# Attention, routing and two feed-forward stages on one core: all queues of the attention loop in source order, not TensorE's alone

## The chip, the core and the metric

One core of a Trainium2 chip runs the whole program. Its engines have an instruction queue each: TensorE (matrix products and transposes, PE in the profile), VectorE (DVE), ScalarE (ACT), GpSimd (POOL) and SyncE (SP), which here only issues DMA and is the load queue. The metric is the time of one execution on the device in microseconds; lower is better.

## What is computed

The reference, cut to what matters (inputs in float32; 4 batches, 8 heads, 576 positions, head size 64):

```python
scores = scale * np.matmul(q, k.transpose(0, 1, 3, 2))
mask = (rel >= 0) & (rel < 64)              # rel = query position - key position
scores = np.where(mask, scores, -1000000000.0)
attn = np.exp(scores - np.max(scores, axis=-1, keepdims=True))
attn = attn / (np.sum(attn, axis=-1, keepdims=True) + 1e-09)
out = np.matmul(attn, v)                    # to rows: 2304 tokens x 512
...
noisy = x @ w_gate + np.log1p(np.exp(x @ w_noise)) * noise
# two best of 8 experts for each token, softmax over the two
out[mask] += top2_w[mask, k, None] * (np.maximum(x[mask] @ w1[e], 0.0) @ w2[e])
...
h = x @ w_in
out = (h * np.clip(h + 3.0, 0.0, 6.0) / 6.0) @ w_out
```

## The kernel before

The program has three parts: an attention loop with the routing of the first tokens woven in (about the first 135 us), the expert stage, and the feed-forward stage.

**The attention loop.** Two heads form a pair; there are 16 pairs of (batch, two heads). Each pair's 576 queries are cut into 9 chunks of 64, and three chunks make a group: 48 groups, numbered g, with n = g // 3 the pair and j = g % 3. A query sees at most its own chunk of keys and the one before. Around a group the loop body calls, in this order:

- `normalise` (odd g): VectorE takes the sums out of `pv`, inverts them (`rs`, L299, L300) and writes the scaled rows into `xbuf` (L304).
- `bg`: one step from a list `fill` of work for routing (below).
- `transposes(g)`: TensorE turns the exponentials `pb` of group g into `pt` (L255, three of them; one buffer).
- `exps(g + 1)`: ScalarE, three exponentials of the scores `s` with the negated maximum `mx` as bias (L247).
- `pt_copy(g)`: ScalarE copies `pt` to `ptb` (L260).
- `tr_half`: when j > 0, TensorE turns q or k of pair n + 2 (L212; two `tr` buffers), and ScalarE and VectorE copy them out (`qbd`, L220 and L222; `kt`, L226).
- `scores(g + 2)`: TensorE adds the mask and the products of q and k into `s` (L235, L239; two buffers), VectorE reduces the maximum `mx` (L241).
- `values(g - 2, g - 1)` (even g): TensorE, `ptb` times v into `pv` (L285).
- `bg` again, then `load_pair(n + 3)` on SyncE (q, k, v: L169, L172, L174; three buffers for q and k, four for v), `odd_slots(n + 2)` on GpSimd (the shifted copy of v, L156), and, for pairs 8 to 15 when j is 2, `w0q.step()`.

**Routing in the loop.** When a batch's heads are done, `gate_batch` adds a chain of steps to `fill`: each token tile is stored to `x_rows` (SyncE, L313), turned on TensorE (L316) and copied by ScalarE (`xT`, L318); then the products with the gate weights (L338), a copy `lt` on VectorE (L344), a turn back (L347), Exp and Ln on ScalarE (L355, L360) between small steps on VectorE (L354 to L370), the search for the two best (L375, L377), the place of each token (TensorE, L390 to L393, and a third Exp, L400), and pairs of one-hot tiles on VectorE (`pa`, L421; `pbt`, L422) whose products TensorE sums (L430). Two batches (token tiles 0 to 3 and 4 to 8) run whole within the loop, in the source at groups 13 to 26 and 27 to 41; then GpSimd gathers the first rows of expert 0 (L506) and TensorE turns them (L532, `build`) in group 45; the third batch begins in group 46 and ends in the expert stage.

**Weights of expert 0.** `w0q` holds eight weights, 512 KB each. A step settles the weight before (VectorE, low half = raw minus high half, L585), loads up to two ahead into two buffers `wraw` (SyncE, L567 or L571), and makes the next high half (GpSimd, L581). The eight steps stand at groups 26, 29, ... 47; the last low half (`lza`) is settled behind the loop. The expert stage begins with eight sums of twelve products each (L891 to L893) over the four weights `hwa`, `hxa`, `hya`, `hza`, then `hh` (ScalarE, L898) and `hl` (VectorE, L899).

**What sets the order.** The program is scheduled by a list scheduler: outside of a manual section it issues on each engine whichever instruction is ready first by its own estimates, source order deciding between ready ones. Inside `tc.manual_schedule(engines=...)` the engines named issue in the order of the source. The attention loop stands in such a section for TensorE alone; the set-up ahead of it stands in none; from the end of the loop on, a second section covers all engines:

```python
        w0q.step()
    order = ctx.enter_context(ExitStack())
    order.enter_context(tc.manual_schedule())
```

The two sections are separate: in the profile, products of the expert stage stand ahead of the last step of the loop's section on TensorE.

Of the kernel before, what the change touches and what calls it, by code (L numbers as in the profile page):

```python
# [40 lines left out]
def ap_of(t, offset, dims):  # L41
    return bass.AP(tensor=t.tensor, offset=t.offset + offset, ap=dims)
# [3 lines left out]
def attention_moe_kernel(ctx, tc, q, k, v, w_gate, w_noise, noise, w1, w2, w_in, w_out, out):  # L46
# [130 lines left out]
    def odd_slots(n):  # L177

        if n < NP:
            t = VT[n]  # L180
            pcopy(t[0:64, 1:8:2], t[64:128, 0:8:2])
            pcopy(t[64:128, 1:7:2], t[0:64, 2:8:2])
# [18 lines left out]
    def tr_half(n, which, a):  # L201
        if n >= NP:
            return
        raw = RAW[n, which]
        if n == 0 and which == "rk":
            tr = aps.tile([128, 3, 2, D + 1], F32, name="pv", bufs=2).rearrange("p c h n -> p (c h n)")
        else:
            tr = ps.tile([128, 512], F32, name="tr", bufs=2)
        r0, r1 = ((0, 4), (4, 6))[a]
        m, t0 = 96 * (r1 - r0), 96 * r0  # L210
        for r in range(r0, r1):
            pe.transpose(tr[:, 96 * (r - r0):96 * (r - r0) + 96], raw[:, r].rearrange("p h d -> p (h d)"), ident[0:96, 0:96])  # L212
        if which == "rq":

            t = QBD[n] = qbds[n % 2]
            for h in range(2):
                o = t[64 * h:64 * h + 64, t0 // 64:(t0 + m) // 64, h]
                i = tr[64 * h:64 * h + 64, 0:m].rearrange("p (c i) -> p c i", i=64)
                if a == 0:
                    act.activation(o, i, AF.Copy, scale=0.125)  # L220
                else:
                    dve.tensor_scalar(o, i, 0.125, None, op0=OP.mult)  # L222
        else:
            if a == 0:
                KT[n] = apool.tile([128, S], F32, name="kt", bufs=2)
            act.copy(KT[n][:, t0:t0 + m], tr[:, 0:m])  # L226
# [5 lines left out]
    def scores(g):  # L232
        n, cs = GROUPS[g]
        s = SC[g] = aps.tile([128, 3, 128], F32, name="s", bufs=2)
        pe.matmul(s, ident16, masks[:, 0:3] if cs[0] == 0 else masks[:, 1:4], start=True, stop=False)  # L235
        for i, c in enumerate(cs):
            l = QBD[n][:, c].rearrange("p h i -> p (h i)")
            k0 = 64 * max(c - 1, 0)
            pe.matmul(s[:, i, :], l, KT[n][:, k0:k0 + 128], start=False, stop=(i == 2))  # L239
        MX[g] = apool.tile([128, 3], F32, name="mx", bufs=3)  # L240
        dve.tensor_reduce(MX[g], s, axis=AX.X, op=OP.max, negate=True)  # L241

    def exps(g):
        n, cs = GROUPS[g]
        PB[g] = apool.tile([128, 3, 128], F32, name="pb", bufs=2)
        for i, c in enumerate(cs):
            act.activation(PB[g][:, i, :], SC[g][:, i, :], AF.Exp, bias=MX[g][:, i:i + 1])  # L247
# [40 lines left out]
    def normalise(g):  # L288
        n, cs = GROUPS[g]
        j = g % 3  # L290
        if j == 0:
            return
        b, p = divmod(n, HP)
        t0, odd = place_of(n, 0)
        pv = PV.pop((n, j - 1))
        m = 3 if j == 1 else 2
        spans = [(0, 1, 64, 128), (1, 3, 0, 128)] if odd and j == 1 else [(0, m, 0, 128)]
        rs = apool.tile([128, 3, 2], F32, name="rs", bufs=2)
        dve.tensor_scalar(rs[:, 0:m], pv[:, 0:m, :, D], 1e-9, None, op0=OP.add)  # L299
        dve.reciprocal(rs[:, 0:m], rs[:, 0:m])  # L300
        for u, w, lo, hi in spans:
            x0 = (t0 + 3 * (j - 1) + u) % (NT // 2)
            assert all(t < NT // 2 or t - NT // 2 in XT for t in range(t0 + 3 * (j - 1) + u, t0 + 3 * (j - 1) + w))
            dve.tensor_tensor(xbuf[lo:hi, x0:x0 + w - u, :, p].rearrange("q t (h a) y -> q t h a y", h=2),  # L304
                              pv[lo:hi, u:w, :, 0:D].rearrange("q t h (a y) -> q t h a y", a=2),
                              rs[lo:hi, u:w, :, None, None].to_broadcast([hi - lo, w - u, 2, 2, 32]), op=OP.mult)
# [194 lines left out]
    def gather(e, m):  # L501
        if e == 0:
            t = XG[e, m] = mp.tile([128, DM], F32, name="xg", bufs=4)
            early = m < SUBS[0][1]
            ix = idx0[:, m:m + 1] if early else idx[:, e, m:m + 1]
            pool.indirect_dma_start(out=t, out_offset=None,  # L506
                                    in_=xrows[0:128 * DONE[KNOWN][0]] if early else xrows,
                                    in_offset=bass.IndirectOffsetOnAxis(ap=ix, axis=0))
            return
        t = XG[e, m] = mp.tile([128, 4, 128], F32, name="xg", bufs=4)  # L510
        for i in range(4):
            pool.indirect_dma_start(out=t[:, i], out_offset=None, in_=pieces(xrows),  # L512
                                    in_offset=bass.IndirectOffsetOnAxis(ap=idx4[:, i, e, m:m + 1], axis=0))
# [26 lines left out]
    def build(e, m):  # L540
        if e == 0:
            s = int(m >= SUBS[0][1])
            turn_rows(XG[e, m], *columns(e, s), 128 * (m - SUBS[s][0]))
        elif m == 2:

            turn(XG[e, m], (*columns(e, 0), 0), (*columns(e, 1), 0))
        else:
            s = int(m > 2)
            turn(XG[e, m], (*columns(e, s), 64 + 128 * (m - 3 * s)))
# [98 lines left out]
    def bg(*kinds, n=1):  # L648

        while fill and n and fill[0][0] in kinds:  # L650
            f = fill.pop(0)[1]
            n -= 1
            if f:
                f()

    with tc.manual_schedule(engines={mybir.EngineType.PE}):
        for which in ("rq", "rk"):
            for a in range(2):
                tr_half(0, which, a)
        scores(0)  # L660
        odd_slots(1)
        scores(1)
        exps(0)

        for g in range(NG + 2):
            n, j = divmod(g, 3)
            for past in ((g - 3, g - 2) if g > 2 and g % 2 else ()):
                normalise(past)
                m, jj = divmod(past, 3)
                b, p = divmod(m, HP)  # L670
                if p == HP - 1 and jj == 2 and b < B - 1:
                    t = gate_batch(DONE[b], lambda: gps.tile([128, 512], F32, name="g"))
                    if b == B - 2:
                        cut = [f for _, f in t].index(None) + 5
                        t, late = t[:cut], [f for _, f in t[cut:] if f]
                    coming += t
                    if b == KNOWN - 1:
                        coming += [(None, None), (None, hold)]
                        coming += [(None, lambda m=m: gather(0, m)) for m in range(SUBS[0][1])]
                        coming += [(None, None)] * 2  # L680
                        coming += [("tr", lambda m=m: build(0, m)) for m in range(SUBS[0][1])]
            bg(None, "tr" if j == 0 else None)
            if g < NG:
                transposes(g)
            if g + 1 < NG:
                exps(g + 1)
            if g < NG:
                pt_copy(g)
            if g == 0:
                for which in ("rq", "rk"):  # L690
                    for a in range(2):
                        tr_half(1, which, a)
            elif j:
                which = ("rq", "rk")[j - 1]
                tr_half(n + 2, which, 0)
                tr_half(n + 2, which, 1)
            if g + 2 < NG:
                scores(g + 2)
            if g and g % 2 == 0:
                values(g - 2, g - 1)  # L700
                bg("col", n=2)
            fill += coming
            del coming[:]
            bg(None, "tr")
            if j == n % 2:
                load_pair(n + 3)
                if n == 1:
                    for w, s in ((w_gate, 0), (w_noise, E)):
                        for a in range(4):
                            sp.dma_start(wg[:, a, s:s + E], ap_of(w, 32 * a * E, [[128 * E, 4], [E, 32], [1, E]]))  # L710
            if j == 2:
                odd_slots(n + 2)
                if 8 <= n < 16:
                    w0q.step()
        while fill:
            bg(None, "tr", "col", n=len(fill))
        w0q.step()
# [535 lines left out]
```

## Time and profile before

| | |
|---|---|
| time, median of 3 runs | 1007.74 us (1007.71 to 1011.16) |
| profiled execution: time / span from first to last instruction | 1008.23 / 1006.5 us |
| granted TensorE clock, mean over the span | 0.996 |
| busy: TensorE / VectorE / ScalarE / GpSimd | 981.5 / 568.0 / 465.6 / 327.4 us |

An engine's busy time is the time in which it has an instruction under way; a granted clock of 1.00 is the full clock. An instruction's idle time stands in brackets behind its row, with what ended it. Times in rows count from the start of the span.

### The profile page before, as it was taken

To read this page: it belongs to the slowest core of one execution; us is meant where nothing else is said; L and a number is where in the kernel's file an instruction comes from. 1 tells how busy PE (TensorE), PEld (TensorE's weight loads), DVE (VectorE), ACT (ScalarE), POOL (GpSimd) and SP (SyncE) were. 2 spreads that over 40 slices of the span, in tenths; PEclk is the share of its full clock that TensorE was granted. 3 is DMA by queue.
4 is the path that set the end of the run, shared out by engine and by line. 5 is a ranking of instruction groups with operands and counts; after the bars stand their busy time and mean duration, and the time that the engine had idled before them with its cause. 6 is when DMAs were issued, how large, how long until landed. Compare 5 with 4: busy or idle time off the path is not lost.

```text
span 1006.5 us, 17395 instructions
## 1 busy us (share of the span) xinstructions
PE 981.5 (98%) x6422; PEld 891.0 (89%) x6422; DVE 568.0 (56%) x1398; ACT 465.6 (46%) x1034; POOL 327.4 (33%) x351
## 2 busy tenths in 40 slices
PE   8988998999999999999999999999999999999998
PEld 7978886998988989999998988989988998899997
DVE  5577965656768686666667656444333433344322
ACT  6857751534444454454454546434333433334333
POOL 2133103732435334242431276732344234410000
PEclk9989999999999999999999999999999999999999
DMA  9899242546656566656666464200111002100000
GB/s 169 180 226 226 78 138 63 179 118 209 211 162 204 195 175 189 195 177 218 203 195 203 144 195 129 70 24 17 58 32 48 24 24 64 27 27 21 11 11 23
DMA packets 116394, 122.42 MB, mean 122 GB/s; under 512 B 69840, under 2 KB 78288, under 8 KB 116304
## 3 DMA queue, kind: packets, MB, share of 16 engines
q1 hardware_dynamic: 96144, 86.17, 31.3%
q0 software_dynamic: 9488, 19.94, 7.1%
q10 hardware_dynamic: 10672, 15.15, 4.2%
q8 instruction: 51, 0.84, 0.4%
q14 instruction: 39, 0.32, 0.1%
HBM read 92.91 MB, written 28.31 MB: 120 GB/s over the span
## 4 chain that ended last, share of the span: by engine, by line
PE 80%; DVE 8%; DMA 5%; issue 3%; ACT 2%; POOL 1%; SPq 0%; ACTq 0%; DVEq 0%; POOLq 0%
PE ph L1192 6%; PE ph L1191 6%; PE ph L1190 6%; PE ph L891 6%; PE ph L892 6%; PE ph L893 6%; PE py L1213 5%; PE py L1212 5%; PE py L1211 5%; PE py L911 4%; PE py L912 4%; PE py L913 4%; PE s L239 2%; PE pv L285 2%; PE pt L255 2%
## 5 line engine op out<-in xcount | busy, mean ns | idle before, releaser
L512 POOL DMA_INDIRECT xg<-x_rows,idx x140 | 146.5, 1047 | 220.2 <-DVE xt L523 168.7
L947 POOL DMA_INDIRECT xg<-y_rows,rows x144 | 145.7, 1012 | 221.9 <-DVE xg L955 76.3
L1195 DVE SCALAR_TENSOR_TENSOR g<-g,ph 128x384 f32<-128x384 f32 (+1 forms) x112 | 55.7, 497 | 159.2 <-ACT g L1194 155.4
L1194 ACT ACTIVATE g<-ph,three 128x384 f32<-128x384 f32 (+1 forms) x112 | 60.0, 535 | 101.2 <-PE ph L1192 98.5
L899 DVE SCALAR_TENSOR_TENSOR hl<-ph,hh 128x320 fp32r<-128x320 f32 (+2 forms) x128 | 60.9, 486 | 77.1 <-ACT hh L898 77.1
L1200 DVE TENSOR_TENSOR hl<-g,hh 128x384 fp32r<-128x384 f32 (+1 forms) x112 | 56.1, 501 | 58.9 <-ACT hh L1198 56.0
L898 ACT ACTIVATE hh<-ph 128x320 fp32r<-128x320 f32 (+2 forms) x128 | 54.3, 435 | 65.2 <-PE ph L893 61.9
L1198 ACT CAST hh<-g 128x384 fp32r<-128x384 f32 (+1 forms) x112 | 52.4, 468 | 63.6 <-DVE g L1195 63.6
L517 ACT CAST xh<-xt 128x512 fp32r<-128x512 f32 (+1 forms) x60 | 33.5, 570 | 81.9 <-DVE xt L523 81.5
L518 DVE TENSOR_TENSOR xl<-xt,xh 128x512 fp32r<-128x512 f32 (+1 forms) x60 | 37.2, 630 | 39.5 <-ACT xh L517 39.5
L247 ACT ACTIVATE pb<-s,mx 128x128 f32<-128x128 f32 x144 | 42.2, 368 | 10.5 <-DVE mx L241 6.5
L156 POOL TENSOR_SCALAR vt<-vt 64x520 f32<-64x520 f32 (+1 forms) x32 | 19.5, 609 | 67.9 <-DMA vt<-in_v_dram 25.7
L239 PE MATMUL s<-kt,qbd 128*128 128x128 f32 x288 | 41.2, 281 | 0.2 <-ACT kt L226 0.2
L239 PEld LDWEIGHTS s<-kt,qbd 128*128 128x128 f32 x288 | 39.8, 197 | 0.8 <-ACT kt L226 0.5
L241 DVE TENSOR_REDUCE mx<-s 128x3 f32<-128x384 f32 x48 | 26.6, 554 | 22.1 <-PE s L239 17.1
L523 DVE STREAM_TRANSPOSE xt<-xg 128x512 f32<-128x512 f32 x53 | 37.4, 706 | 0.4
L750 DVE SCALAR_TENSOR_TENSOR na<-mag,raw 128x256 f32<-128x256 f32 x64 | 26.8, 419 | 12.1 <-DMA w_out<-na 5.1
L747 ACT ACTIVATE mag<-raw 128x256 f32<-128x256 f32 x64 | 27.5, 430 | 12.5 <-DVE na L756 12.5
L756 DVE CUSTOM_DVE_ANT_0 na<-mag,nr 128x512 uint16<-128x512 uint16 x64 | 27.3, 426 | 9.5 <-ACT hh L898 0.5
L919 ACT COPY y<-py 128x512 f32<-128x512 f32 x33 | 19.2, 583 | 27.4 <-PE py L913 18.2
L260 ACT COPY ptb<-pt 128x384 f32<-128x384 f32 x48 | 23.2, 484 | 12.7 <-PE pt L255 12.6
L755 DVE SCALAR_TENSOR_TENSOR mag<-na,mag 128x256 int32<-128x256 int32 x64 | 27.3, 426 | 2.2
(517 smaller groups left out, 3172.2 us busy)
## 6 DMA issues: line engine op xcount, KB each, us to landing
wraw<-in_moe_w_dram SPq DMA_DIRECT2D x60, 512.0 KB
y_rows<-y ACTq DMA_DIRECT2D x40, 256.0 KB
raw<-in_moe_w_in_dram SPq DMA_DIRECT2D x32, 256.0 KB
raw<-in_moe_w_out_dram SPq DMA_DIRECT2D x32, 256.0 KB
rq<-in_q_dram SPq DMA_DIRECT2D x32, 144.0 KB
rk<-in_k_dram SPq DMA_DIRECT2D x32, 144.0 KB
x_rows<-xbuf SPq DMA_DIRECT2D x18, 256.0 KB
out_dram<-y ACTq DMA_DIRECT2D x17, 256.0 KB
```

Of the source, the lines that this page charges most:

```text
L239: pe.matmul(s[:, i, :], l, KT[n][:, k0:k0 + 128], start=False, stop=(i == 2))
L512: pool.indirect_dma_start(out=t[:, i], out_offset=None, in_=pieces(xrows), in_offset=bass.IndirectOffsetOnAxis(ap=idx4[:, i, e, m:m + 1], ...
L891: pe.matmul(p, wh[:, fs], xh[:, d, :n], start=(d == 0), stop=False)
L892: pe.matmul(p, wh[:, fs], xl[:, d, :n], start=False, stop=False)
L893: pe.matmul(p, wl[:, fs], xh[:, d, :n], start=False, stop=(d == 3))
L899: dve.scalar_tensor_tensor(hl[f][:, cs], p, 0.0, hh[f].bitcast(F32)[:, cs], op0=OP.max, op1=OP.subtract)
L947: pool.indirect_dma_start(out=g[:, r], out_offset=None, in_=pieces(left), in_offset=bass.IndirectOffsetOnAxis(ap=rows4[:, r, tt, j:j + 1], ...
L1190: pe.matmul(p, wh[:, c], xh[:, d, :n], start=(d == 0), stop=False)
L1191: pe.matmul(p, wh[:, c], xl[:, d, :n], start=False, stop=False)
L1192: pe.matmul(p, wl[:, c], xh[:, d, :n], start=False, stop=(d == 3))
L1194: act.activation(g, p, AF.Relu, bias=three)
L1200: dve.tensor_tensor(gl[f], g, gh[f].bitcast(F32), op=OP.subtract)
```

## The change

All engines and SyncE issue the instructions of the attention loop in the order of the source. Before, this held for TensorE alone. Nothing is added or taken out.

```diff
-    with tc.manual_schedule(engines={mybir.EngineType.PE}):
+    with tc.manual_schedule():
         for which in ("rq", "rk"):
             for a in range(2):
                 tr_half(0, which, a)
```

## Rows read from the trace of the kernel before

**Rows 1.** The page, busy time, share of the span and instructions.

```profile
PE 981.5 (98%) x6422; PEld 891.0 (89%) x6422; DVE 568.0 (56%) x1398; ACT 465.6 (46%) x1034; POOL 327.4 (33%) x351
```

**Rows 2.** Windows: length, busy time (instructions) of PE, PEld, DVE, ACT, POOL, clock, DMA share, GB/s.

```profile
45.79:84.25 38.46, 33.34 (x404) 30.46 (x403) 30.30 (x107) 24.39 (x72) 14.22 (x18) 0.91 1.02 240
84.25:128.00 43.75, 40.50 (x562) 37.34 (x561) 35.62 (x133) 32.18 (x96) 8.90 (x12) 1.00 0.53 125
128.00:176.00 48.00, 43.32 (x413) 36.16 (x412) 29.29 (x146) 15.74 (x39) 7.72 (x9) 1.00 0.29 98
176.00:1006.50 830.50, 822.66 (x4568) 748.90 (x4566) 446.10 (x930) 360.18 (x732) 287.35 (x279) 1.00 0.38 115
53.53:60.35 6.82, 6.16 (x33) 5.87 (x35) 2.76 (x11) 2.78 (x9) 0.66 (x2) 0.50 0.87 199
```

**Rows 3.** TensorE's timeline: start, length, instruction, count, idle before.

```profile
18.58 0.55 PE L255 MATMUL pt<-ident,pb 128*128 128x128 f32 x3
...
39.31 0.55 PE L255 MATMUL pt<-ident,pb 128*128 128x128 f32 x3
...
54.19 0.47 PE L347 MATMUL g<-ident,lt 128*128 128x128 f32 x1 [2.65 <-DVE lt L344]
```

**Rows 4.** VectorE's timeline, 48 to 54 us.

```profile
48.34 1.23 DVE L585 TENSOR_TENSOR lwa<-wraw,hwa 128x1024 fp32r<-128x1024 f32 x1 [2.44 <-POOL hwa L581]
...
49.95 0.72 DVE L222 TENSOR_SCALAR qbd<-tr 64x192 f32<-64x192 f32 x2
...
51.97 1.23 DVE L585 TENSOR_TENSOR lxa<-wraw,hxa 128x1024 fp32r<-128x1024 f32 x1 [0.71 <-POOL hxa L581]
53.11 0.15 DVE L299 TENSOR_SCALAR rs<-pv 128x4 f32<-128x4 f32 x1
...
53.85 0.28 DVE L344 COPY lt<-g 128x128 f32<-128x128 f32 x1
```

**Rows 5.** The load queue's timeline, SyncE.

```profile
21.65 2.41 SPq L710 DMA_DIRECT2D wg<-in_moe_w_gate_dram  x4
...
37.82 1.58 SPq L567 DMA_DIRECT2D wraw<-in_moe_w_dram  x3
```

**Rows 6.** ScalarE's timeline, 14 to 15 us.

```profile
14.41 0.48 ACT L260 COPY ptb<-pt 128x384 f32<-128x384 f32 x1 [0.63 <-PE pt L255]
14.79 0.89 ACT L247 ACTIVATE pb<-s,mx 128x128 f32<-128x128 f32 x3
```

**Rows 7.** VectorE by line, 45.79 to 128 us: busy us, mean ns of one | idle before.

```profile
L241 DVE TENSOR_REDUCE mx<-s 128x3 f32<-128x384 f32 x30 | 16.6, 552 | 7.9 <-PE s L239 7.2 <-ACT pb L247 0.3
...
L585 DVE TENSOR_TENSOR lzb<-wraw,hzb 128x1024 fp32r<-128x1024 f32 x1 | 1.9, 1927 | 0.0
...
L585 DVE TENSOR_TENSOR lya<-wraw,hya 128x1024 fp32r<-128x1024 f32 x1 | 1.2, 1225 | 0.0
```

**Rows 8.** GpSimd's timeline at 96 us.

```profile
96.13 1.04 POOL L581 TENSOR_SCALAR hza<-wraw 128x1024 fp32r<-128x1024 f32 x1 [0.73 <-DMA wraw<-in_moe_w_dram]
```

**Rows 9.** TensorE's timeline, from the loop's end into the expert stage.

```profile
135.69 1.06 PE L338 MATMUL g<-xT,wg 128*32 128x128 f32 x26 [0.33 <-ACT xT L318]
...
138.97 0.28 PE L893 MATMUL ph<-xh,lza 128*128 128x256 f32 x1
...
152.93 0.61 PE L430 MATMUL g<-pbt,pa 128*128 128x144 f16 x2 [1.69 <-DVE pbt L422]
```

**Rows 10.** VectorE's timeline, steps of the third gating batch.

```profile
139.40 0.19 DVE L354 TENSOR_SCALAR zc<-g 128x32 f32<-128x32 f32 x1 [2.32 <-PE g L347]
...
140.10 0.19 DVE L364 SCALAR_TENSOR_TENSOR gd<-gu,ge 128x32 f32<-128x32 f32 x1
140.91 0.35 DVE L365 RECIPROCAL gu<-gu 128x32 f32<-128x32 f32 x1 [0.61 <-ACT gl L360]
...
142.43 0.37 DVE L375 MAX8 tm<-gd 128x8 f32<-128x8 f32 x4
...
143.38 0.22 DVE L382 TENSOR_TENSOR oh<-iota,ti 128x64 f32<-128x64 f32 x1
```

## The prediction

> **What bounds the kernel now.** I read the page first: TensorE is busy for 98% of the span [rows 1]. The windows by stage show where the other 2% lies [rows 2]. From 176 us to the end TensorE is busy in 822.66 of 830.50 us, and that part already issues in source order on every engine. What the change can move lies before it. In the attention loop a group (three query chunks of one pair of heads) is recognised in TensorE's timeline by its three transposes of L255: group 3 starts them at 18.58, group 13 at 39.31 [rows 3], so an undisturbed group takes 20.73 / 10 = 2.07 us. The windows are cut where groups 15 and 28 start theirs (45.79, 84.25) and at the first transpose of gathered rows, L532 (128.00) [rows 2]: groups 15 to 27, where the first gating batch runs, take 38.46 / 13 = 2.96. TensorE idles 38.46 - 33.34 = 5.1 us there and 43.75 - 40.50 = 3.3 us in the next stretch [rows 2]. [...]
>
> [...]
>
> **What the change does, part by part.** TensorE's order stays. On the other queues I count positions in the source and put row durations on them; each engine goes on when its own last instruction and its inputs are done. No operation is added or taken away.
>
> *Start (groups 1, 2).* ScalarE now copies `ptb` of group 1 at 14.41 (0.48 us) and starts the exponentials of group 2 at 14.79 (0.89 us) [rows 6]. In the source the exponentials of g+1 stand ahead of the copy of g, and `pt` has one buffer, so the transposes of group 2 wait for the copy: +0.45 us, bounds 0 and 0.9. Later groups lose nothing: from the end of one score product, reduction 0.55 + exponentials 0.89 + copy 0.48 + three hops of about 0.1 is some 2.2 us, about what an undisturbed group takes [rows 3, 6, 7], and before it needs the result TensorE has a group's products.
>
> *Groups 15 to 27.* Five of the eight low halves run here now (48.34 and 51.97 are two of them); in source order none does. VectorE's 30.30 us of work become 30.30 - 5 x 1.225 = 24.2 [rows 2, 7], and TensorE's 33.34 become 33.34 - 3.1 = 30.3 if the clock holds. Waits that source order keeps or adds, walked queue by queue: the copy of token tile 2 ahead of the exponentials of group 16, 0.45; L338 to `lt` to L347, 0.5 instead of 2.65; in group 18 the exponentials stand behind Exp and Ln of the gate, which wait for VectorE twice, 0.7; in groups 19 and 20 VectorE has the seven gate steps L364 to L370 (140.10 to 142.43 less a wait of 0.61, 1.7), two normalisations (0.74 and more), the top-2 search (142.43 to 143.38, 0.95) and the query copy (0.72) between two reductions [rows 4, 10], some 5 us where TensorE has about 3, and two score buffers hide part, 1.1; in group 21 the exponentials of group 22 stand behind the gate's third Exp, which waits for a normalisation on VectorE, 1.45. Together 4.2, so 34.5 us for 38.46: **-4.0 us**. Bounds: -7.0 if only the first two waits stay, 0 if these waits double.
>
> *Groups 28 to 45.* Here three low halves run now; in source order six do (groups 29, 32, 35, 38, 41, 44), so VectorE's 35.62 us become 39.3 [rows 2, 7], against 40.50 of TensorE: both full. Waits: 0.5 for the turn of tile 8; 0.35 for the gate's Exp and Ln in group 32; then, five tiles wide instead of four, 1.8 us of gate steps and 1.1 of search, 1.2 of low half and 1.0 of normalisation stand between two reductions, 5.1 us where TensorE has 2.4, which costs 1.75 in group 34 and 35 and 1.35 in 36, where the gate's Exp again stands ahead; 0.6 in group 40; 1.0 before L532, since VectorE writes the gather's indices only after it has come through its line. That is 5.55, so 46.05 us for 43.75: **+2.3 us**. Bounds: -2 (TensorE's 40.50 and only the first and last wait) and +8 (the waits double).
>
> *Contention.* While GpSimd made `hza` (96.13, 1.04 us) the low half `lzb` took 1.93 us instead of 1.225 [rows 7, 8]. From group 26 on GpSimd has seven weight steps in source order, VectorE is then the tighter line, and I take one to two such overlaps: +1.0, bounds 0 and four of them, 2.8. [...]
>
> *Tail.* The last step in the source is the low half of the eighth weight, `lza`, behind the gate steps of the third batch. Today GpSimd makes its high half at 96.13 [rows 8], some 40 us ahead of the use of `lza` at 138.97, the last product of d = 3 in the expert stage's first sum [rows 9]. The chain now is: L338 ends at 136.75; L347; from `zc` at 139.40 to the end of the gate steps at 142.43 is 3.0 us [rows 10], 2.4 without the 0.61 that VectorE waited for ScalarE, which then had the expert stage's work to do; then 1.225; with hops 4.1 us after L347. If L347 comes right behind its copy, TensorE, which today needs 2.2 us from L338 to that product, stands 2.0 us; if it stays behind the first eleven products, 3.7. Of that the 1.69 us and smaller waits for VectorE at 153 [rows 9] give back some 1 to 2, since VectorE's line then runs ahead: **+1.5**, bounds 0 and 4.1.
>
> *Loads.* The weight loads go from 37.82 [rows 5] to behind group 24, and each now waits in the load queue for the low half that frees its buffer; behind it stand the next pair's q and k. By the positions these still issue about four groups ahead of their transposes, some 8 us, and DMA, which was full in groups 15 to 27 (share 1.02) and half empty after (0.53) [rows 2], evens out. I cost it at 0; the cover is those four groups. The gate weights' eight loads (four of them 2.41 us [rows 5]) now stand behind `vt` of pair 4 and push pair 5's q back by about 1 us, still some 3 us ahead of its transposes: 0 too.
>
> **Sum.** 0.45 - 4.0 + 2.3 + 1.0 + 1.5 = +1.25 us on the profiled execution's 1008.23, so 1009.5; that execution lies 0.5 above the median of the runs, so 1009.0 us.
>
> **Rivals.** *VectorE's line carries less slack than I charge (slower).* Every gate step now stands ahead of a reduction that TensorE waits for. In its favour: VectorE was already busy 35.62 of 43.75 us and gets 3.7 more. Against: the two score buffers. It decides once the waits of groups 28 to 45 nearly double (+7 in place of +2.3), those of 15 to 27 grow by 1 (-3), contention takes 1.5 and the tail pays 3.7: 1007.7 + 0.45 - 3 + 7 + 1.5 + 3.7 = 1017 us.
>
> *The gates come out clean (faster).* If ScalarE and VectorE keep up, groups 15 to 27 take 31.5 us (-7), 28 to 45 lose nothing, and L347 comes early, so the tail is +0.5: 1001.5 us. Against it stand the 5 us lumps above.
>
> *Late loads (slower).* If a q load in groups 30 to 40 takes over 8 us, TensorE waits for it: three pairs at about 2 us each give 1015. Nothing in the trace of before shows TensorE waiting for a load after 10 us.
>
> *A second drop of the clock.* A tail wait of 3.7 us would be longer than the 2.65 us that preceded the drop now; another stretch like it costs 3.1 us: 1012. [...]
>
> *The change does nothing visible*, because the orders differ only where nobody waits: 1007.7. The weight steps alone, 15 groups early, speak against it.
>
> **How the numbers follow.** Forecast, with the clock drop and the no-effect case beside it (all within 0.5%, 5 us, about what a measurement of this kernel tells from no change): 0.57. VectorE too tight 0.24, late loads 0.06, clean gates 0.13. So faster 0.13, same 0.57, slower 0.30. The forecast's own range is 1003 to 1013; to leave out no more than 2 in 10 it reaches to the two main rivals, 1001.5 to 1017.
>
> **What would show it.** Right: no L585 on VectorE before about 84 us, L347 waiting about 0.5 us, no half clock near 53, group 28 some 4 us earlier, L532 about 1.5 us earlier, and TensorE standing 2 to 4 us for `lza` before its first sum ends. Wrong: TensorE waiting for q or k loads, reductions 3 us or more behind their scores from group 20 on, or the expert stage after 176 us changing its length.

## The result, and the profile after

The changed kernel takes 1022.9 us (median of 4 runs, 1019.52 to 1023.73) against 1008.76 us, a ratio of 1.0121 [1.0101, 1.0142]. It is slower, and lies beyond the forecast of 1009.0 and its range. Timed again beside other kernels it came out at 1.013 [1.0106, 1.0154]. The profiled execution took 1019.52 us with a span of 1017.6 us, 11.1 us more than before. It is the fastest of the four: the others were granted a mean clock of 0.992 in place of 0.996, and by (1 - clock) x span, an estimate of what the half clock costs, that is some 4 us more, about what they take longer (3.2 to 4.2 us).

The page's busy line, to be read against [rows 1]:

```profile
PE 984.1 (97%) x6422; PEld 891.4 (88%) x6422; DVE 570.2 (56%) x1398; ACT 463.0 (45%) x1034; POOL 326.4 (32%) x351
```

Windows of the changed kernel, columns as in [rows 2], cut at the same instructions: where groups 15 and 28 start, at L532, and at the product that stood at 176.04 us before.

```profile
47.57:83.24 35.67, 30.44 (x404) 27.51 (x402) 25.27 (x103) 24.08 (x76) 5.46 (x9) 1.00 0.59 140
83.24:131.36 48.12, 41.85 (x560) 37.69 (x561) 39.47 (x133) 30.78 (x95) 13.57 (x17) 1.00 0.73 164
131.36:185.42 54.06, 45.42 (x411) 37.80 (x412) 32.44 (x149) 15.99 (x39) 9.37 (x10) 0.97 0.35 113
185.42:1017.60 832.18, 823.19 (x4567) 748.67 (x4566) 446.09 (x930) 360.06 (x732) 286.50 (x279) 1.00 0.38 114
8.42:11.83 3.41, 3.41 (x17) 3.34 (x18) 0.99 (x2) 0.88 (x3) 1.14 (x2) 0.50 1.32 212
148.37:151.78 3.41, 3.41 (x19) 3.41 (x18) 0.42 (x1) 1.25 (x3) 0.00 (x0) 0.50 0.34 133
```

The same cuts in a second profile of the changed kernel (e5 below, span 1016.7 us), with its half-clock stretches:

```profile
46.11:81.70 35.59, 30.45 (x404) 27.51 (x402) 25.17 (x103) 24.13 (x76) 5.51 (x9) 1.00 0.60 143
81.70:131.25 49.55, 43.62 (x561) 38.89 (x561) 39.73 (x133) 30.85 (x95) 13.83 (x17) 0.97 0.69 160
131.25:186.33 55.08, 46.52 (x411) 38.93 (x412) 32.35 (x149) 16.01 (x39) 9.45 (x10) 0.94 0.33 111
186.33:1016.70 830.37, 822.19 (x4567) 748.75 (x4566) 446.68 (x930) 360.25 (x732) 286.82 (x279) 1.00 0.37 115
104.85:108.26 3.41, 3.09 (x16) 2.69 (x15) 2.01 (x7) 2.38 (x9) 1.05 (x1) 0.50 1.13 172
145.81:152.64 6.83, 5.90 (x27) 5.90 (x28) 2.54 (x16) 1.57 (x4) 0.00 (x0) 0.50 0.26 79
```

Set against [rows 2], the two profiles give the change of each stretch in us. In the half-clock stretch at 148.37 TensorE starts the products of L891 to L893 as closely as 0.21 us apart (149.19 to 150.04), just behind it 0.12 us apart (152.01 to 152.36). By the granted clock of 0.50, an estimate, a stretch of 3.41 us in which TensorE is busy throughout holds 1.7 us of work at full clock, so it costs up to 1.7 us:

| stretch | forecast | first profile | second profile |
|---|---|---|---|
| start to group 15 | +0.45 | +1.78 (half clock at 8.42) | +0.32 |
| groups 15 to 27 | -4.0 | -2.79 | -2.87 |
| group 28 to L532 (contention included) | +3.3 | +4.37 | +5.80 (half clock at 104.85) |
| L532 into the expert stage, 48.04 before | +1.5 | +6.02 (half clock at 148.37) | +7.04 (twice as long, at 145.81) |
| the rest, 830.46 before | 0 | +1.7 | -0.1 |
| sum | +1.25 | +11.1 | +10.2 |

Up to L532 the change loses 3.36 and 3.25 us, in the stretch behind it 6.0 and 7.0. The +1.7 us of the rest in the first profile is not there in the second. TensorE's waits by cause (instruction, what it waited for, us in total, times, longest), first groups 15 to 27, then 28 to L532, then the stretch behind:

```profile
PE pt L255 <- ACT ptb L260: 2.5, 4, 1.2
PE tr L212 <- DVE qbd L222: 2.2, 2, 1.6
PE g L347 <- DVE lt L344: 0.4, 1, 0.4
...
PE pt L255 <- ACT ptb L260: 3.5, 7, 1.5
PE tr L212 <- DVE qbd L222: 0.9, 1, 0.9
...
PE ph L893 <- DVE lza L585: 3.8, 1, 3.8
PE g L430 <- DVE pbt L422: 2.0, 3, 1.6
```

The long wait for `lt` of [rows 3] is gone (2.65 to 0.42): the low halves `lwa` and `lxa`, ahead of `lt` on VectorE in [rows 4], now start at 89.2 and 100.3 us. In its place stand many for ScalarE's `ptb`, three for VectorE's `qbd`, and one of 3.81 us for `lza`. TensorE's timeline at the ones that matter:

```profile
54.00 0.33 PE L347 MATMUL g<-ident,lt 128*128 128x128 f32 x1 [0.42 <-DVE lt L344]
...
62.81 0.36 PE L212 MATMUL tr<-ident,rk 96*128 96x96 f32 x2 [1.59 <-DVE qbd L222]
...
67.97 0.55 PE L255 MATMUL pt<-ident,pb 128*128 128x128 f32 x3 [1.25 <-ACT ptb L260]
...
108.92 0.55 PE L255 MATMUL pt<-ident,pb 128*128 128x128 f32 x3 [1.55 <-ACT ptb L260]
...
142.78 0.27 PE L347 MATMUL g<-ident,lt 128*128 128x128 f32 x1
146.87 0.39 PE L893 MATMUL ph<-xh,lza 128*128 128x256 f32 x1 [3.81 <-DVE lza L585]
...
162.33 0.24 PE L430 MATMUL g<-pbt,pa 128*128 128x144 f16 x1 [1.62 <-DVE pbt L422]
```

VectorE's timeline shows what the wait for `lza` consists of: the gate's steps from L354 on, which need L347, and behind them the low half. The last three rows lead to the wait for `pbt` at L430.

```profile
143.09 0.19 DVE L354 TENSOR_SCALAR zc<-g 128x32 f32<-128x32 f32 x1 [2.20 <-PE g L347]
...
145.38 0.19 DVE L370 TENSOR_TENSOR gd<-gd,g 128x32 f32<-128x32 f32 x1
145.59 1.23 DVE L585 TENSOR_TENSOR lza<-wraw,hza 128x1024 fp32r<-128x1024 f32 x1
...
152.31 0.42 DVE L899 SCALAR_TENSOR_TENSOR hl<-ph,hh 128x256 fp32r<-128x256 f32 x1 [3.20 <-ACT hh L898]
153.94 0.42 DVE L344 COPY lt<-py 128x256 f32<-128x256 f32 x1 [1.20 <-PE py L341]
...
161.96 0.31 DVE L422 TENSOR_SCALAR pbt<-iotab,cf,tokid 128x144 f16<-128x144 f16 x1
```

ScalarE's timeline shows a wait for `ptb` being made: the gate's third Exp (L400) stands first and waits for VectorE, and the exponentials and the copy come behind it.

```profile
66.58 0.21 ACT L400 ACTIVATE gw<-gw 128x4 f32<-128x4 f32 x1 [1.38 <-DVE gw L399]
66.69 0.86 ACT L247 ACTIVATE pb<-s,mx 128x128 f32<-128x128 f32 x3
67.44 0.48 ACT L260 COPY ptb<-pt 128x384 f32<-128x384 f32 x1
```

### The profile page after: what moved, and what is told of

Same layout as the page of the kernel before. It is cut to its first block, busy times and chain, and to the rows that moved or that the text cites. A ratio compares the mean times of both kernels' runs of the same rounds, so it can differ in the third digit from the quotient of the medians.

```text
span 1017.6 us, 17347 instructions
## 1 busy us (share of the span) xinstructions
PE 984.1 (97%) x6422; PEld 891.4 (88%) x6422; DVE 570.2 (56%) x1398; ACT 463.0 (45%) x1034; POOL 326.4 (32%) x351
## 4 chain that ended last, share of the span: by engine, by line
PE 78%; DVE 10%; DMA 5%; ACT 4%; issue 2%; SPq 0%; ACTq 0%; POOL 0%; DVEq 0%
PE ph L1192 6%; PE ph L1190 6%; PE ph L1191 6%; PE ph L891 6%; PE ph L892 6%; PE ph L893 6%; PE py L1213 5%; PE py L1212 5%; PE py L1211 5%; PE py L911 5%; PE py L912 5%; PE py L913 5%; DMA wraw<-in_moe_w_dram 2%; PE s L239 2%; PE pv L285 1%
## 5 line engine op out<-in xcount | busy, mean ns | idle before, releaser
L239 PE MATMUL s<-kt,qbd 128*128 128x128 f32 x288 | 41.2, 280 | 0.2 <-ACT kt L226 0.2
L239 PEld LDWEIGHTS s<-kt,qbd 128*128 128x128 f32 x288 | 39.6, 196 | 0.8 <-ACT kt L226 0.5
L255 PE MATMUL pt<-ident,pb 128*128 128x128 f32 x144 | 25.3, 285 | 6.3 <-ACT ptb L260 6.3
L893 PE MATMUL ph<-xh,lza 128*128 128x320 f32 (+2 forms) x80 | 24.9, 312 | 3.8 <-DVE lza L585 3.8
```

What stands on the lines that cost most here:

```text
L893: pe.matmul(p, wl[:, fs], xh[:, d, :n], start=False, stop=(d == 3))
```

## The experiments

Four sets of four kernels, each set with its own runs of the kernel before. In the second set the kernel before took 1007.91 us; in the other three it took 1043.0 to 1045.0 us, with half-clock stretches in the expert stage of every profile (mean granted clock 0.984 in place of 0.995), so ratios are compared, not times.

| kernel | issued in source order | `lza` moved | ratio [95%] |
|---|---|---|---|
| e5 | all | no | 1.0130 [1.0106, 1.0154] |
| e1, e9 | all | yes | 1.0072 [1.0046, 1.0098], 1.0076 [1.0049, 1.0103] |
| e2 | TensorE, VectorE | no | 1.0049 [1.0023, 1.0075] |
| e8 | TensorE, VectorE | yes | 1.0009 [0.9994, 1.0023] |
| e3 | TensorE, ScalarE | no | 1.0063 [1.0031, 1.0094] |
| e14 | TensorE, VectorE, ScalarE | yes | 1.0074 [1.0051, 1.0097] |
| e4 | TensorE, SyncE | no | 1.0067 [1.0035, 1.0099] |
| e7 | all but ScalarE | yes | 1.0011 [0.9992, 1.0030] |
| e15 | all; from group 28 not ScalarE | yes | 1.0046 [1.0021, 1.0071] |
| e16 | all but ScalarE; from group 28 all | yes | 1.0020 [0.9997, 1.0044] |
| e6 | all, third Exp later | yes | 1.0082 [1.0060, 1.0105] |
| e10 | all, `ptb` first | yes | 1.0060 [1.0034, 1.0086] |
| e11 | all, both | yes | 1.0062 [1.0038, 1.0086] |
| e12 | all, both, weights earlier | yes | 1.0104 [1.0065, 1.0143] |
| e13 | all, low halves on GpSimd | yes | 1.0128 [1.0090, 1.0167] |

**The tail: e1, e5, e9.** The last settling step is moved ahead of what is left of the routing list:

```diff
+        w0q.step()
         while fill:
             bg(None, "tr", "col", n=len(fill))
-        w0q.step()
```

> The changed kernel with one instruction moved: the low half of the eighth weight (lza, L585) stands on VectorE ahead of the gate steps of the third batch (before lt, L344) instead of behind them. Theory (the tail is a chain that hangs on the place of lza): the wait of 3.81 us before L893 goes, and with it the half clock that followed (some 1.5 us): about 5.5 us less than the changed kernel, ratio to the kernel before 1.006 to 1.007. Rival (something else is late at the same place, the gate chain or the weight's load): the product waits for it nearly as long, at most 1.5 us gained, ratio 1.011.

> The changed kernel once more, beside the next three, so that they share a chip and the runs of the kernel before with it. Expected 1.012 (1.010 to 1.014), as measured first; and in its trace again about 3.8 us of TensorE standing for lza ahead of L893, with a half-clock stretch just behind it. Rival: on a chip whose granted clock is lower the waits cost differently, and the ratio comes out at 1.007 or less, in which case the kernel with the low half moved (1.007) had not shown that the tail matters.

> The changed kernel with the last low half moved ahead of the third gating batch, once more, as the base of the next three on one chip. Expected 1.007 (1.005 to 1.009): some 5 us below the changed kernel (1.0121 and 1.013). Rival: the tail is worth less on this chip, 1.010 or more.

The wait ahead of L893 is gone in e1 and e9, it is 3.80 us in e5, and the ratio falls from 1.0121 and 1.013 to 1.0072 and 1.0076. That is about 0.005, 5 us, of which 3.8 are the wait. So the theory of the chain holds, but not its second half: the half clock did not go with the wait. e1 and e9 have one later, beside the wait for `pbt` at L430 (up to 158.44 and 158.59 us), and that wait is 1.61 to 1.62 us in all three, with the tail or without it. Windows of e1, then of e9:

```profile
160.21:163.62 3.41, 3.41 (x34) 3.22 (x34) 2.89 (x16) 0.59 (x2) 0.00 (x0) 0.50 0.00 0
158.39:165.22 6.83, 6.44 (x47) 5.87 (x48) 5.73 (x33) 0.59 (x2) 0.00 (x0) 0.50 0.00 0
```

The 1 us that the wait does not explain lies within the intervals.

**One engine at a time: e2, e3, e4, e8.** Only the line of the section differs:

```diff
-    with tc.manual_schedule():
+    with tc.manual_schedule(engines={mybir.EngineType.PE, mybir.EngineType.DVE}):
```

In e3 `Activation` (ScalarE) stands in place of `DVE`, in e4 `SP` (SyncE); e8 is e2 with the last low half moved as in e1.

> The loop's section covers TensorE and VectorE; ScalarE, GpSimd and the load queue go by the scheduler as before. Theory (VectorE's order carries the loss: the tail's lza behind the gate steps, and gate steps ahead of reductions in groups 19 to 36): ratio 1.009 to 1.012, wait before L893 lza of 3 us or more. Rival (ScalarE's order carries the loop's part, since the changed kernel's waits of the transposes name the copy ptb behind the exponentials): only the tail is left, ratio about 1.005.

> The loop's section covers TensorE and ScalarE. Theory (VectorE's order carries the loss): only the start's copy of ptb behind the exponentials and a few tenths behind the gate's Exp and Ln, ratio 1.001 to 1.003. Rival (ScalarE's order carries the loop's part): ratio 1.006 or more, with transposes waiting for ptb in groups 18 to 22 and 33 to 36 as in the changed kernel.

> The loop's section covers TensorE and the load queue. Theory (early weight steps cost the kernel before the wait for lt and the clock drop behind it, and late ones cost nothing as long as VectorE may take them when it likes): no half clock near 53 us, 3 to 5 us less than before, ratio 0.995 to 0.997. Rival (loads behind the weights' buffers come late): TensorE waits for rq or rk in groups 30 to 40 or for lza at the end, ratio 1.003 or more.

> The section names TensorE and VectorE, and the last low half stands ahead of the third batch. VectorE and TensorE alone gave 1.0049 with a wait of 3.81 us for lza. Theory (that tail is all that VectorE's order by itself costs): no wait for lza, and 0.999 to 1.000. Rival (the loss of VectorE's order lies in the loop, and the tail is made up for later): 1.004 to 1.006.

VectorE's order by itself costs the tail and no more: 1.0049 with a wait of 3.81 us for `lza`, 1.0009 without it. L532 then starts at 127.65 us in e2 and 126.39 in e8, against 128.00 before. ScalarE's order alone costs 0.006, as the rival said, but not by the waits that it named: in e3 the longest are 2.86 and 2.45 us for `lt` and 1.90 for `mk`, all three VectorE's, and 2.50 for `ptb`. The load queue's order alone was to gain 0.003 to 0.005 and loses 0.007. It does take out the drop of the clock near 53 us (L347 waits 0.41 us), and groups 15 to 27 take 30.67 us in place of 38.46. But the stretch from there to L532 takes 54.46 us in place of 43.75: waits of 1.0 to 1.6 us appear between 83 and 104 us, for `qbd`, `xT`, `lt` and `ptb`, and one of 1.8 us at 115.03. I had no theory for those, and no run took them apart.

One thing limits these four runs. The engines that a section leaves out do not keep their order of before, since the scheduler orders them anew around it: VectorE makes `lwa` at 48.34 us before [rows 4], at 44.98 in e3 and at 80.4 in e4, and its other instructions change places too. So e3 and e4 price a section together with what the scheduler makes of the rest, and not one queue alone.

**All but ScalarE: e7, e14.** The section names PE, DVE, SP and Pool in e7, and PE, DVE and Activation in e14; both have the last low half moved.

> The section names TensorE, VectorE, SyncE and GpSimd, that is all but ScalarE, and the last low half stands ahead of the third batch. Theory (ScalarE's order is what turns VectorE's lumps into waits of the transposes for ptb; the weight steps and loads in source order by themselves take out the wait and the half clock at 53 us): ptb waits of 1 us and more are gone, no half clock near 53, and the ratio is 0.996 to 1.000. Rival (the loss sits in VectorE's source order, whatever ScalarE does, for instance the 1.6 us wait for qbd at 62.8 us and the low halves beside GpSimd's): 1.004 to 1.007.

> The section names TensorE, VectorE and ScalarE; SyncE and GpSimd are left to the scheduler; the last low half moved. VectorE alone gave 1.0009, all engines 1.0072 to 1.0076, all but ScalarE 1.0011. Theory (ScalarE waits in its order for VectorE, and VectorE in its order for what TensorE then does late: the two together make the loss): 1.006 to 1.008. Rival (it takes the load queue's and GpSimd's order too, which put the low halves late): 1.001 to 1.004.

Leaving ScalarE alone to the scheduler takes 1.0072 and 1.0076 down to 1.0011, just above the 0.996 to 1.000 expected. Leaving SyncE and GpSimd to it in place of ScalarE takes nothing off (e14, 1.0074). So with VectorE in source order ScalarE's order costs about 0.006. e7's waits of TensorE from 47 to 83 us, to be set against the first three rows of the changed kernel's waits above:

```profile
PE tr L212 <- ACT kt L226: 1.1, 2, 0.6
PE tr L212 <- ACT qbd L220: 0.6, 2, 0.3
PE g L347 <- DVE lt L344: 0.4, 1, 0.4
```

The waits for `ptb` are gone, and so are those for VectorE's `qbd`, though VectorE's own order is the same: 2.1 us in place of 5.1.

**Where in the loop: e15, e16.** The section is closed and opened again at group 28, e15 so, and e16 with the two lists of engines exchanged:

```diff
-    with tc.manual_schedule():
+    with ExitStack() as section:
+        section.enter_context(tc.manual_schedule())
...
         for g in range(NG + 2):
+            if g == 28:
+                section.close()
+                section.enter_context(tc.manual_schedule(engines={mybir.EngineType.PE, mybir.EngineType.DVE, mybir.EngineType.SP, mybir.EngineType.Pool}))
             n, j = divmod(g, 3)
```

> All engines in the section up to group 27; from group 28 on all but ScalarE; the last low half moved. Theory (the loss is made where VectorE's line is full, from group 28 on: in the trace of the changed kernel group 28 still started 1.0 us earlier than before, and L532 3.4 us later): 1.001 to 1.003. Rival (ScalarE's lateness comes from groups 1 to 27, where it costs 3 to 4 us against what the clock and the freed VectorE give, and the later groups only keep it): 1.004 to 1.007.

> The reverse: all but ScalarE up to group 27, all engines from group 28 on; the last low half moved. Theory (loss from group 28 on): 1.004 to 1.007. Rival (loss from groups 1 to 27): 1.001 to 1.003. If both this and its reverse come out near 1.004, the loss is spread over both stretches.

I expected the loss from group 28 on. The early half costs more: above e7's 1.0011, 0.0035 for groups 1 to 27 and 0.001 for the later ones. The intervals overlap, so what stands is that the later groups alone do not make the loss. Their profiles agree on groups 15 to 27: e15 has the 2.5 us for `ptb` and 2.1 for VectorE's `qbd`, e16 has neither.

**Mending two positions on ScalarE: e6, e10, e11.** e6 moves the third Exp to the end of the next step, e10 the copy ahead of the exponentials, e11 does both:

```diff
-            act.activation(w[:, :, 1], w[:, :, 1], AF.Exp)
             dve.tensor_copy(expt[:, t0:t0 + n], T["ti"][:, :, 0:2])
...
             dve.scalar_tensor_tensor(qf, bf, -128.0, pn, op0=OP.mult, op1=OP.add)
+            act.activation(T["gw"][:, :, 1], T["gw"][:, :, 1], AF.Exp)
...
+            if g < NG:
+                pt_copy(g)
             if g + 1 < NG:
                 exps(g + 1)
-            if g < NG:
-                pt_copy(g)
```

> The changed kernel with the last low half moved ahead of the third gating batch, and with the gate's third Exp (L400) called at the end of the next step (s5) instead of inside s4, so that in groups 21 and 36 the exponentials of the next group no longer stand behind it on ScalarE. Theory (the third Exp, which waits for a normalisation on VectorE, is what the two longest ptb waits of the loop come from, 1.25 us at 67.97 and 1.55 us at 108.92): both waits fall under 0.4 us and the ratio is 0.002 to 0.003 below that of the kernel with the low half moved alone (1.0072): about 1.0045. Rival (VectorE's line is late there anyway, the reduction of the same group stands behind the normalisation and the same gate steps): the waits stay or come back at the next group, and the ratio stays at 1.006 to 1.008.

> As the kernel before, and pt_copy(g) is called ahead of exps(g + 1), so that on ScalarE the copy that frees pt no longer stands behind the next group's three exponentials. ScalarE's order has been shown to cost 0.006 when all other engines issue in source order (1.0072 against 1.0011). Theory (most of it is this one position: every time VectorE's maximum is late, the exponentials are, and with them ptb): ratio 0.002 to 0.004 below the kernel with the low half moved alone, 1.003 to 1.005; the waits for ptb at groups 2, 19 and 33 to 35 are gone. Rival (it is the steps of the gate and of tr_half on ScalarE, which stand ahead of both): no change, 1.006 to 1.008.

> Both moves on ScalarE: pt_copy ahead of the exponentials, and the gate's third Exp called at the end of the next step; the last low half moved as well. Theory (these two positions are what ScalarE's order costs): 1.001 to 1.003, about that of the kernel without ScalarE in the section (1.0011). Rival (the third Exp alone gave no lower time, 1.0082, since TensorE waits for VectorE a group later anyway): the same as with pt_copy moved alone.

The named waits go as expected: in e6 group 22 starts its transposes without one, and in e11 no wait of TensorE for `ptb` of half a microsecond is left. The time does not follow: 1.0082, 1.0060 and 1.0062. In e11 TensorE waits later for VectorE, and VectorE has no idle time from 105 us to then. TensorE's row, then VectorE's:

```profile
115.86 0.35 PE L212 MATMUL tr<-ident,rk 96*128 96x96 f32 x2 [2.12 <-DVE qbd L222]
```

```profile
110.76 0.55 DVE L241 TENSOR_REDUCE mx<-s 128x3 f32<-128x384 f32 x1
...
113.29 0.42 DVE L304 TENSOR_TENSOR xbuf<-pv,rs 128x256 f32<-128x256 f32 x1
113.63 1.03 DVE L453 TENSOR_SCALAR gw<-gw 128x5 f32<-128x5 f32 x1
114.70 0.19 DVE L454 RECIPROCAL gates<-gw 128x5 f32<-128x5 f32 x1
114.92 0.17 DVE L455 TENSOR_TENSOR gates<-gw,gates 128x5 f32<-128x5 f32 x1
115.00 0.71 DVE L222 TENSOR_SCALAR qbd<-tr 64x192 f32<-64x192 f32 x2
115.75 0.56 DVE L241 TENSOR_REDUCE mx<-s 128x3 f32<-128x384 f32 x1
```

From one reduction (110.76) to the next (115.75) VectorE runs 5.0 us of one-hot tiles, two normalisations, gate weights and the copy of q in source order. The first theory, that two positions on ScalarE are what its order costs, has fallen: e10 and e11 lie 0.0014 to 0.0016 below e9, which is within the intervals. Of the 5.0 us, L453 holds 1.03 where it takes 0.17 elsewhere; it ends 0.03 us after the high half `hxb` that GpSimd makes beside it (113.59 to 114.63).

**Relieving VectorE: e12, e13.** e12 is e11 with the weight steps at pairs 4 to 12; e13 is e1 with the low halves made by GpSimd:

```diff
-                if 8 <= n < 16:
+                if 4 <= n < 13:
...
-    w0q = Halves(expert_weights(0))
+    w0q = Halves(expert_weights(0), pool)
```

> As the kernel before, and the weight steps stand at pairs 4 to 12 instead of 8 to 15 and behind the loop, so that the low halves fall into groups 17 to 38 in place of groups 29 to 47 and the last is settled in the loop. Theory (with ScalarE's two positions mended, what is left is VectorE's line between 99 and 128 us, which in source order has six low halves and their overlaps with GpSimd where the kernel before had three; the VectorE-only kernel lost 5 us there): 0.997 to 1.000, and L532 starts 2 us or more earlier. Rival (moved forward, the steps meet the first gating batch and put the wait and the half clock of 53 us back): 1.002 or more, with a wait of 1 us or more between 45 and 70 us.

> The changed kernel with the last low half moved, and all eight low halves of expert 0 made by GpSimd in place of VectorE (same order, same positions). Theory (VectorE's line in groups 28 to 45 is full, 27 of 29 us, and any lateness there stays): some 7 us of work leave VectorE, TensorE's waits for qbd and ptb between 99 and 128 us fall below 0.6 us each, L532 starts 2 to 4 us earlier, ratio 1.002 to 1.005. Rival (what counts is the order on ScalarE, or GpSimd's slower low halves hold back VectorE's two-input operations as long as they took there): 1.007 or more.

Both are slower, as their rivals said. e12 waits 1.33 us for `pb` at 60.00 us and 1.52 us for `qbd` at 117.13; L532 starts at 133.97 us. In e13 the longest waits of the loop stay above 1 us, and its profile has 10.24 us of half clock from 107.14 on. GpSimd takes 2.35 us for a low half, and VectorE pays for some of it. VectorE's rows, then GpSimd's:

```profile
101.64 2.18 DVE L369 TENSOR_TENSOR gd<-gd,noise 128x40 f32<-128x40 f32 x1
...
109.01 2.01 DVE L397 TENSOR_TENSOR macc<-macc,msum 128x8 f16<-128x8 f16 x1
```

```profile
101.42 2.35 POOL L585 TENSOR_TENSOR lya<-wraw,hya 128x1024 fp32r<-128x1024 f32 x1
...
108.65 2.35 POOL L585 TENSOR_TENSOR lwb<-wraw,hwb 128x1024 fp32r<-128x1024 f32 x1
```

Each of the two small operations, 0.19 and 0.16 us long elsewhere in this trace, ends within 0.05 us of GpSimd's (103.82 beside 103.77, 111.02 beside 111.00). So part of the work taken off VectorE came back as longer operations there, by 1.99 and 1.85 us. That this makes e13 slow is not shown: by (1 - clock) x span its runs lose 21.4 us to the clock on average and those of e14, in the same set, 17.0, and that is 4.4 of the 4.5 us between the two means. This run does not tell what a lighter VectorE would bring.

## Why the prediction failed

**The tail, mis-sized.** The mechanism was right: chain, instructions and place. The wait of 3.81 us is the 3.7 that the prediction gave for L347 behind the first eleven products, where it stayed. The step that failed is the next one, that 1 to 2 us would be given back at L430 because VectorE's line then runs ahead. That wait is 1.62 us, 1.69 before [rows 9]. VectorE comes to `pbt` there behind other gate steps and behind `hl`, which needs TensorE's own sums: it stands idle 3.20 us up to 152.31 and 1.20 us up to 153.94, so its line shifts with TensorE's and has no lead. The sum's 1.5 moreover lay between the cases of 2.0 and 3.7 us; with 3.7 alone the same give-back leaves 1.7 to 2.7. The other part is the clock: "a second drop" stood among the rivals at 3.1 us, but inside the forecast, and its cost was not in the sum. It came in both profiles, for 3.41 and 6.83 us, up to 1.7 and 3.4. Wait and clock make nearly all of the +6.0 and +7.0 that stand in place of +1.5. Moving one call took TensorE's idle time there from 8.64 us (54.06 - 45.42) to 4.95 in e1 and 4.56 in e9, and left the half clock.

**Groups 15 to 27, nearly.** The two gains are there: TensorE's busy time is 30.44 for a forecast of 30.3, VectorE's 25.27 for 24.2, and no half clock stands near 53 us. The 3.1 us that the forecast takes off TensorE's time is half of the 6.16 us in the half-clock row of [rows 2], an estimate by its clock of 0.50; 2.90 came off (33.34 - 30.44). The waits were to be 4.2 us: 0.5 at L347 (0.42), 0.7 in group 18 (0.69), 1.1 in 19 and 20 (1.59), 1.45 in group 21 (1.25), 0.45 in group 16 behind the copy of tile 2 (0.28, a wait for `ptb`). Those five sum to 4.23 us. TensorE idles 5.23: what the walk lacked are small waits at the end of the stretch, 0.57 and 0.20 us for `qbd` and 0.23 for `ptb`.

**Groups 28 to 45, low by 1.1 and 2.5.** Forecast were 5.55 us of waits and 1.0 of contention, 6.55; TensorE idles 48.12 - 41.85 = 6.27. The rest is TensorE's busy time, 41.85 us where the same instructions took 40.50 at the same clock; the second profile has 43.62 with a half-clock stretch. I took it to stay. The instructions themselves hardly lengthen (L255 takes 280 ns in the mean before and 284 after, L239 274 and L285 225 in both); their lengths add up to 139.1 us before and 138.8 after, so TensorE's instructions overlap, and what shrank is this overlap. Why it did, no run took apart.

**Start.** +0.32 us in the profile without a half-clock stretch there, in the forecast's 0 to 0.9, with the wait where it was expected (0.34 us for `ptb` ahead of group 2 at 15.89); +1.78 with one.

**Loads** took nothing: none of TensorE's waits in these stretches is for a load of q or k, and the rival of late loads is out. **VectorE too tight** was the nearest rival (1017), with the right sign, but its main term, +7 in groups 28 to 45, did not come. Its 3.7 us in the tail did.

**What the walk by waits hid.** I added up VectorE's and ScalarE's waits by place and gave most to VectorE's lumps. The runs show that VectorE's order costs 0.001 once the tail is mended, and that ScalarE's beside it costs 0.006. TensorE's idle time from group 15 to L532 shows about 4 of these 6 us: 12.05 us in e1 and 12.20 in e9, 7.94 in e7. Up to L532 the changed kernel stands at +3.36 and +3.25 us; without ScalarE's order it is 126.39 - 128.00 = -1.6 in e8 and 129.37 - 128.00 = +1.4 in e7, the latter with two half-clock stretches on the way (13.12 and 101.86, 3.41 us each). The whole is then 0.006 for ScalarE's order, 0.005 for the tail and 0.001 for the rest, 0.012 as measured. With the clock's share taken out of each mean by (1 - clock) x span, an estimate, the kernels lie above the kernel before by 11.3 us (e5), 6.2 and 6.5 (e1, e9), 2.4 and 2.5 (e7, e8): 5 for the tail, 4 for ScalarE's order, and 2.4 for the rest, which e7 and e8 hide behind a better clock. Whether the order brings that clock about, no run shows.

**Open.** Which of ScalarE's positions make the 0.006: mending the two that the waits named returned about 0.0015, no more than the noise, while the lateness reappeared at VectorE's `qbd`; its copies of q, k and token tiles, which also stand ahead of exponentials, were not tried. Why the load queue's order alone costs 0.007, and nothing that shows in e7, is open too; the new orders of VectorE and ScalarE in e4 are a rival that was not tested. No kernel tried is faster than the one before; the nearest, e8, is level with it.

## What to carry to other kernels

An instruction order written for one engine is not an order for the others: in this kernel, with one `pt` buffer between TensorE and ScalarE, the third Exp's wait of 1.38 us (up to 66.58) was passed on to the exponentials and the copy behind it, and reached TensorE as 1.25 us for `ptb` (67.97). Look first for the last call of the section: a low half that was done some 35 us ahead of its use (103.9 us, used at 138.97) became the end of a chain of 4 us merely by standing behind steps that need a late product. A wait named in a trace is not a cost until an experiment that removes it also moves the time.

## What the hardware showed

**VectorE and GpSimd.** The prediction took its +1.0 from one overlap, in which `lzb` took 0.70 us more than `lya` [rows 7, 8]. In the changed kernel three of VectorE's operations end no earlier than the high half that GpSimd makes beside them. The first and the third read two tiles, the second one tile and columns of scalars. VectorE's rows, then GpSimd's:

```profile
106.48 0.79 DVE L397 TENSOR_TENSOR macc<-macc,msum 128x8 f16<-128x8 f16 x1
...
122.61 1.04 DVE L422 TENSOR_SCALAR pbt<-iotab,cf,tokid 128x144 f16<-128x144 f16 x1
...
130.01 2.06 DVE L585 TENSOR_TENSOR lyb<-wraw,hyb 128x1024 fp32r<-128x1024 f32 x1
```

```profile
106.22 1.04 POOL L581 TENSOR_SCALAR hwb<-wraw 128x1024 fp32r<-128x1024 f32 x1 [3.63 <-DMA wraw<-in_moe_w_dram]
...
122.52 1.08 POOL L581 TENSOR_SCALAR hyb<-wraw 128x1024 fp32r<-128x1024 f32 x1 [2.83 <-DMA wraw<-in_moe_w_dram]
...
129.97 1.04 POOL L581 TENSOR_SCALAR hzb<-wraw 128x1024 fp32r<-128x1024 f32 x1 [0.53 <-DMA wraw<-in_moe_w_dram]
```

The first ends at 107.27, GpSimd's at 107.26; it takes 0.16 us elsewhere, so it loses 0.63. The second ends at 123.65, GpSimd's at 123.60, and loses 0.73 (0.31 elsewhere). The third takes 0.84 us more than the 1.225 of [rows 7]. With e13's 2.18 and 2.01 us, the loss in these five overlaps is a little less than what was left of GpSimd's operation when VectorE's started: 0.63 of 0.78 us, 0.73 of 0.99, 0.84 of 1.00, and in e13 1.99 of 2.13 and 1.85 of 1.99. The 0.70 us of [rows 7, 8], of 0.85 left, lies among the first three.

What the prediction left out is that the kernel before has more such overlaps than one. By what VectorE's operations take there above the shortest of their kind (where it is over 0.2 us), they cost VectorE 2.6 us in groups 15 to 27 and 1.7 from there to L532 before, 0.5 and 2.6 in the changed kernel. So the +1.0 that the prediction charged to the second stretch came on VectorE (+0.9), and 2.1 us that no term held went from the first.

**The clock.** One program did not draw the same clock each time. In the second set the mean granted clock of the kernel before ran from 0.991 to 0.998 over its runs. Half-clock stretches moved: the changed kernel has them at 8.42 and 148.37 us in one profile, at 104.85 and 145.81 in the other. The one at 8.42 follows no long wait: in the 7 us before it TensorE's longest is 0.69 us. Over that set, (1 - clock) x span is 5.4 us for the kernel before (0.9946 of 1005.7) and 7.3 for the changed one (0.9928 of 1018.9), so by this estimate the clock accounts for 1.9 of the 13.2 us between them.
